# First layer of seven of nine token tiles as seven block products per pair of chunks instead of eight

## The chip, the cores and the metric

The kernel runs on one core of a Trainium2 chip. The metric is the device time of one execution in microseconds (us). Beside the times there is a profile of one execution, taken on the same core. The engines are TensorE (PE; its weight loads are shown as PEld), VectorE (DVE), ScalarE (ACT), GpSimd (POOL) and SyncE (SP), which here only issues DMAs.

## The reference

Banded attention over 8 batches, 8 heads, 576 positions and a head width of 64, then a two-layer network over all 4608 tokens. All is float32.

```
scores = (q @ k.T) / sqrt(64)
mask   = (0 <= pos_q - pos_k) & (pos_q - pos_k < 64)
attn   = softmax(where(mask, scores, -1e9))
x      = (attn @ v) as [4608 tokens, 512]
h      = x @ w_in                                  # 512 -> 2048
g      = h if h >= 1, 0 if h <= -1, else (h + 1)**2 / 4
out    = g @ w_out                                 # 2048 -> 512
```

## The kernel before

**Split operands.** Each float32 operand of a large matmul is kept as a high part and a low part that the array takes at full rate (type F32R), and a product is three matmuls: high times high, high times low, low times high. So every "block product" below is three matmuls for each 128 rows of the contraction.

**Tiles.** The tokens go in nine tiles of 512. The hidden width of 2048 is cut into NF = 16 chunks f of 128. For a tile t and a chunk f, `ffn_in` (L568) does the first layer: 4 pieces of the contraction times 3 parts = 12 matmuls of 128x512 into one PSUM bank of the pool `ps_h` (2 banks). Then the gate: ScalarE `ffn_relu` (L578) and `ffn_square` (L583), VectorE `ffn_gate` (L590, which reads the bank once more and so frees it), ScalarE `ffn_high` (L595), GpSimd `ffn_low` (L600; on VectorE in tile 0). `ffn_out` (L613) is the second layer: 12 matmuls of 128x512 into four banks `acc` that live for the whole tile. So a chunk is two blocks of 12 matmuls on PE; the blocks of different chunks alternate. In tile 0, in the first chunks of tile 1 and in the last chunk of the last tile some first-layer blocks are cut into halves of 256 columns.

**Attention.** A tile's x comes from four attention steps s of 128 tokens each, which run while the tile before it is in the network: scores on PE (L378, pool `ps_a`), mask and maximum on VectorE (L390, L394), exponentials on ScalarE (L401), division (L413, one head half on VectorE, the other on GpSimd), transposes on VectorE (L422), values on PE (L442), and then the split of x into `xh` and `xl` (L239 or L237, L455). From s = 8 on the scores of a step and the values of the step before it are one piece of work on PE (`joined`), so they stand next to each other.

**Weights.** The weights come in as int64 words holding float64, and are turned into high and low float32 parts once, in tile 0, by a chain on ScalarE and VectorE (L266 to L305). They stay in SBUF for the whole run (one slot `w{f}_{unit}` each).

**What sets the order.** The class `Plan` takes every piece of work with a key (its due time in units of a block), a cost per engine it may run on, what it needs, and which buffers it takes and gives back. It walks through time and gives each engine the next piece; the kernel's instructions are then written in that order. Each engine works through its own list strictly in that order, waiting on semaphores. SP issues all DMAs but the first two.

```
        xi = x_in[t] = add(key, dict(PE=12 * (12.5 + n * .4175)), lambda e, f=f, r=r: ffn_in(t, f, r), ...
        joined = SOON <= s < NT // SB - 1
```

Of the kernel before, what the change touches and what calls it, by code (L numbers as in the profile page):

```python
# [50 lines left out]
FIRST_LOAD = 0, (0,)  # L51
# [31 lines left out]
BUFS = dict(qt=2, kt=2, vt=4, ps_a=2, sm=4, ptd=3, x=2, u=2, ps_h=2, a=2, gh=2, gl=2, acc=4, o=2)  # L83
# [85 lines left out]
def banded_attention_then_ffn(ctx: ExitStack, tc: tile.TileContext, q, k, v, w, masks, out, dims):  # L169
# [4 lines left out]
    NF = w.shape[0]  # L174
# [6 lines left out]
    xpool = ctx.enter_context(tc.tile_pool(name="xpool", bufs=BUFS["x"]))  # L181
# [20 lines left out]
    wpool = ctx.enter_context(tc.tile_pool(name="wpool", bufs=1))  # L202

# [47 lines left out]
    def w_load(g, eng=nc.sync):  # L251
        f, units = g
        m = len(units) * DM
        ws[g] = t = wpool.tile([P, 4 * m], U16, name="raw", tag=f"w{f}_{units[0]}")
        src = w[f, :, units[0]:units[-1] + 1].bitcast(U16)
        eng.dma_start(out=t[:, :4 * m - 1], in_=src.rearrange("p u n -> p (u n)")[:, 1:])  # L256

    def w_sign(g):

        m = len(g[1]) * DM
# [21 lines left out]
    def w_rest(g):  # L284

        m = len(g[1]) * DM
# [8 lines left out]
    def w_high(g, eng):  # L295
        f, units = g
        ws[g] = t = wpool.tile([P, len(units), 2, DM], F32R, name="wts", tag=f"w{f}_{units[0]}")
        for j, u in enumerate(units):
            wts[f, u] = t[:, j]
        us[g] = us[g].bitcast(F32).rearrange("p (u n) -> p u n", n=DM)  # L300
        copy(eng, t[:, :, 0], us[g])
# [7 lines left out]
    def add_weights(f, units):  # L309
        g = f, units  # L310
        m = len(units) * DM
        act, high, join, low, small = 105 + .916 * m, 92 + .844 * m, 10 + 1.22 * m, 67 + 1.05 * m, 90 + .25 * m
        key = f * W_STEP - (W_FIRST[f] if f < len(W_FIRST) else W_LEAD) + .5 * units[0]
        x = add(W0_KEY + W0_STEP * (f + .5 * units[0]), dict(SP=W_LOAD * len(units)), lambda e: None if g == FIRST_LOAD else w_load(g), lag=DMA_LAG)
# [8 lines left out]
        for u in units:  # L323
            w_ready[f, u] = x
# [90 lines left out]
    def att_transpose(s, h, i):  # L415


        sm, pt = blk[s, h][1], ptd[(2 * s + h) % len(ptd)]
        for j in range(QB // SQ):
# [10 lines left out]
    def att_transposed(s, h, eng):  # L430
        copy(eng, ptd[(2 * s + h) % len(ptd)], pts.pop((s, h)))

    def att_values(s, pool):

        vt, pt = [vts.pop((s, i)) for i in range(2)], [ptd[(2 * s + h) % len(ptd)] for h in range(2)]
        vals[s] = ps = banks_of_heads(pool)
        for p in range(NP):
            for i in range(2):
                n = slice(i * QB, (i + 1) * QB)
                for h in range(2):  # L440
                    c = (2 * p + h) * D
                    nc.tensor.matmul(  # L442
                        ps[half[h], p, n], lhsT=vt[i][:, c:c + D], rhs=pt[h][:, p, n], start=True, stop=True
                    )

    def att_high(t, i, eng):
        s = starts[t] // SB + i
        if t not in xt:
            xt[t] = [xpool.tile([P, NP, TMAX], F32R, name=n) for n in ("xh", "xl")]
        copy(eng, xt[t][0][:, :, i * SB:(i + 1) * SB], vals[s])  # L450
# [7 lines left out]
    x_ready, x_first = {}, {}  # L458
    last = dict(s=[], t=[], v=[])

    before = {}

    def add_step(t, i):

        s = starts[t] // SB + i
        masked = s < PE_MASKS
        joined = SOON <= s < NT // SB - 1
# [20 lines left out]
        if s - 1 in before:  # L488
            needs_v, gives_v, split = before.pop(s - 1)

            def do(e):
                att_scores(s, masked, ps)
                att_values(s - 1, "ps_h")
# [14 lines left out]
        for h in range(2):  # L508
# [22 lines left out]
            else:  # L531
                if s >= SOON:
                    due = key + B_DUE[1] + B_DUE[2] * h
                x = add(
                    due, dict(DVE=1890), lambda e, h=h: att_transpose(s, h, 0), [x] + first, takes=["ptd"]
                )
                first = [x]
                taken.append(x)
                x = add(due, dict(DVE=1890), lambda e, h=h: att_transpose(s, h, 1), [x], gives=[("sm", xs, h)])
# [5 lines left out]
        def split(xo, due, pv):  # L545
            after = [xo] if i == 0 else [xo, x_first[t]]
# [11 lines left out]


# [16 lines left out]
    def ffn_relu(t, f, r):  # L576
        gs[t, f, r.start] = [gate_tile("a", F32, r)]
        nc.scalar.activation(gs[t, f, r.start][0], phs[t, f, r.start], AF.Relu, bias=0.5, scale=0.5)  # L578
# [22 lines left out]

    def ffn_out(t, f, r, i0=None):

        _, gh, gl = gs[t, f, r.start]
        for k, i in enumerate(subs(r)):
            if i0 not in (None, i):
                continue
            if f == 0:
                acc[t, i] = bank("acc")
            sub = slice(k * P, (k + 1) * P)  # L610
            for n in pieces(t, i) if f == NF - 1 else [slice(0, DM)]:
                for j, (g, part) in enumerate(((gh, 0), (gh, 1), (gl, 0))):
                    nc.tensor.matmul(  # L613
                        acc[t, i][:, n], lhsT=g[:, sub], rhs=wts[f, 1][:, part, n], start=(f == 0 and j == 0),
                        stop=(f == NF - 1 and j == 2 and n.stop == DM),
# [32 lines left out]

    def parts(t, f):
# [3 lines left out]
        key = step(t) + f * n / 384  # L653
        if t == 1 and f < FRONT:
            return [(r, step(t) + (i * FRONT + f) * m / 384) for i, r in enumerate(halves)]
# [6 lines left out]
    def add_ffn(t):  # L662
        first, before, x_out = {}, [x_in[t - 1]] if t else [], {}
        for f in range(NF):
            for r, key in parts(t, f):
                n = r.stop - r.start
                over = {x_in[t, i] for i in subs(r)} if f else set(before) | {x_ready[t][i] for i in subs(r)}
                last_in = f == NF - 1 and r.stop == TILES[t]
                xi = x_in[t] = add(
                    key, dict(PE=12 * (12.5 + n * .4175)), lambda e, f=f, r=r: ffn_in(t, f, r),  # L670
                    [w_ready[f, 0], *over] + ([x_in[t]] if last_in else []), takes=["ps_h"],
                    gives=[("x", x_first[t])] if last_in else [],
                )
                for i in subs(r):
                    x_in[t, i] = xi
                late = G_LATE if t == 0 else [0] * 5
                xa = add(key + late[0], dict(ACT=70 + n * .83), lambda e, f=f, r=r: ffn_relu(t, f, r), [xi], takes=["a"])
# [4 lines left out]
                    key + late[2], dict(DVE=65 + n * 1.04), lambda e, f=f, r=r: ffn_gate(t, f, r), [xq], gives=[("ps_h", xi)]  # L682
                )
                xh = add(key + late[3], dict(ACT=90 + n * .84), lambda e, f=f, r=r: ffn_high(t, f, r), [xg], takes=["gh"])
# [5 lines left out]
                over = {x_out[i] for i in subs(r)} if f else set()  # L690

                ends = t == len(TILES) - 1 and f == NF - 1 and r.stop == TILES[t]
                for i0 in subs(r) if ends else [None]:
                    xo = add(
                        key + O_LAG, dict(PE=3 * (n / P if i0 is None else 1) * 232), lambda e, f=f, r=r, i0=i0: ffn_out(t, f, r, i0),
                        [xl, w_ready[f, 1], *over], takes=[] if f else ["acc"] * len(subs(r)),
# [24 lines left out]
    for t in reversed(range(len(TILES))):  # L721
        for i in reversed(range(TILES[t] // SB)):
            at, apart = (step(t) - A_LEAD, A_STEP) if t < 2 else (step(t) - A_END - B_STEP, B_STEP if t > 2 else B_FIRST)
# [7 lines left out]
    for f in range(NF):  # L731
        for units in ((0,), (1,)) if f < FINE else ((0, 1),):
            add_weights(f, units)
    for t in range(len(TILES)):
        if t + 1 < len(TILES):
            for i in range(TILES[t + 1] // SB):
                add_step(t + 1, i)
        add_ffn(t)
    with tc.manual_schedule():
# [54 lines left out]
```

## Time and profile before

| | |
|---|---|
| median of 3 runs | 901.85 us (901.27 to 902.82) |
| profiled execution, first to last instruction | 899.2 us |
| what lies around that span, against the median | 2.65 us |
| PE busy | 885.6 us (98%) |
| VectorE, ScalarE, GpSimd busy | 539.3, 452.2, 192.7 us |
| a middle tile (436 to 532 us): PE, VectorE, ScalarE, GpSimd busy | 96.00, 57.65, 43.60, 24.12 of 96 us |
| granted TensorE clock, mean | 0.994 |

The profiled execution has no time of its own other than its span; the table sets the span against the median of the runs. A busy PE need not be PE at its peak, because matmuls overlap in the records; what one costs is read from the distance between the starts of neighbours, which the chain that ended last gives for whole blocks. L numbers are lines of the kernel above.

### The profile page before, as it was taken

What the parts mean: (1) busy time and instruction counts of PE and PEld (TensorE: products, weight loads), DVE (VectorE), ACT (ScalarE), POOL (GpSimd) and SP (SyncE); (2) the same over time, 40 slices, a digit from 0 to 9 for tenths busy, and PEclk for the clock granted to TensorE, in tenths of its full rate; (3) what the DMA queues carried; (4) which work ended last, traced back from release to release, by engine and by line L of the source; (5) the groups of instructions that cost most, each with busy time, mean ns of one, the idle gap of its engine ahead of it and who ended that gap; (6) DMA issues with size and microseconds to landing.
All of it is one profiled execution on the core that took longest, in us unless ns stands there. A gap on an engine that the chain in (4) does not pass through costs nothing.

```text
span 899.2 us, 17299 instructions
## 1 busy us (share of the span) xinstructions
PE 885.6 (98%) x6843; PEld 729.1 (81%) x6843; DVE 539.3 (60%) x1373; ACT 452.2 (50%) x1139; POOL 192.7 (21%) x175
## 2 busy tenths in 40 slices
PE   7899999999999999999999999999999999999997
PEld 6788888888888888888888888888888888888886
DVE  6999996667745666666645574556466666521111
ACT  6999955445534454444444454345344453433333
POOL 1000002222222222222222232222222222222221
PEclk8999999999999999999999999999999999999999
DMA  9991012112201121111211121113011220001001
GB/s 327 403 387 66 25 53 102 53 57 104 100 17 38 53 100 54 53 54 54 101 53 53 55 100 54 43 41 104 20 54 54 80 75 24 2 1 47 1 1 48
DMA packets 29426, 69.95 MB, mean 78 GB/s; under 512 B 3616, under 2 KB 3872, under 8 KB 29344
## 3 DMA queue, kind: packets, MB, share of 16 engines
q1 hardware_dynamic: 29056, 67.92, 21.4%
q8 instruction: 54, 0.88, 0.4%
q10 hardware_dynamic: 288, 0.92, 0.3%
q14 instruction: 28, 0.23, 0.1%
HBM read 59.39 MB, written 9.44 MB: 77 GB/s over the span
## 4 chain that ended last, share of the span: by engine, by line
PE 97%; DMA 1%; DVE 1%; SPq 0%; ACT 0%; issue 0%; ACTq 0%
PE acc L613 44%; PE ps_h L568 43%; PE ps_a L378 4%; PE ps_h L442 3%; DMA raw<-in_w 1%; PE ps_a L442 1%; PE acc L227 0%; PE acc L442 0%; PE ps_a L428 0%; PE ps_h L428 0%; DVE nm L394 0%; ACT sm L401 0%; SPq L256 0%; PE ps_a L372 0%; DVE sm L413 0%; PE acc L378 0%
## 5 line engine op out<-in xcount | busy, mean ns | idle before, releaser
L568 PE MATMUL ps_h<-xh,wts 128*128 128x512 f32 (+1 forms) x1200 | 380.2, 382 | 1.8 <-DVE a L590 0.9
L613 PE MATMUL acc<-wts,gh 128*128 128x512 f32 x1154 | 360.5, 394 | 0.0
L600 POOL TENSOR_TENSOR gl<-a,gh 128x512 fp32r<-128x512 f32 (+1 forms) x131 | 167.4, 1278 | 686.8 <-ACT gh L595 579.3
L590 DVE SCALAR_TENSOR_TENSOR a<-a,ps_h 128x512 f32<-128x512 f32 (+1 forms) x150 | 99.9, 667 | 285.3 <-ACT a L583 255.1
L568 PEld LDWEIGHTS ps_h<-xh,wts 128*128 128x128 f32 x1200 | 222.9, 188 | 46.3 <-DVE a L590 1.3
L613 PEld LDWEIGHTS acc<-wts,gh 128*128 128x128 f32 x1154 | 213.4, 188 | 45.4 <-issue 0.3
L568 PE MATMUL ps_h<-xl,wts 128*128 128x512 f32 (+1 forms) x600 | 228.6, 381 | 0.7 <-DVE xl L455 0.7
L578 ACT ACTIVATE a<-ps_h 128x512 f32<-128x512 f32 (+1 forms) x150 | 87.1, 581 | 275.8 <-PE ps_h L568 273.2
L422 DVE STREAM_TRANSPOSE ptd<-sm 32x128 f32<-32x128 f32 x696 | 210.7, 303 | 23.3 <-POOL sm L413 12.6
L613 PE MATMUL acc<-wts,gl 128*128 128x512 f32 x577 | 224.5, 389 | 0.0
L595 ACT CAST gh<-a 128x512 fp32r<-128x512 f32 (+1 forms) x150 | 90.4, 603 | 105.9 <-DVE a L590 96.3
L568 PEld LDWEIGHTS ps_h<-xl,wts 128*128 128x128 f32 x600 | 113.0, 188 | 22.3 <-DVE xl L455 0.9
L613 PEld LDWEIGHTS acc<-wts,gl 128*128 128x128 f32 x577 | 108.4, 188 | 23.5 <-DVE gl L600 0.2
L401 ACT ACTIVATE sm<-sm,nm 128x96 f32<-128x96 f32 (+1 forms) x256 | 93.4, 369 | 38.6 <-DVE nm L394 38.6
L583 ACT ACTIVATE a<-a 128x512 f32<-128x512 f32 (+1 forms) x148 | 91.1, 616 | 4.7
L401 ACT ACTIVATION_READ_ACCUMULATOR sm<-sm,nm 128x1 f32 x256 | 48.7, 190 | 0.0
L378 PEld LDWEIGHTS ps_a<-kt,qt 64*32 64x32 f32 (+1 forms) x2016 | 27.7, 109 | 11.8 <-issue 10.9
L394 DVE TENSOR_REDUCE nm<-sm 128x4 f32<-128x384 f32 (+1 forms) x64 | 35.8, 561 | 0.9
L378 PE MATMUL ps_a<-kt,qt 64*32 64x96 f32 (+1 forms) x2016 | 35.3, 253 | 0.0
L390 DVE SCALAR_TENSOR_TENSOR sm<-ps_a,nmsk 128x384 f32<-128x384 f32 x58 | 31.7, 548 | 0.9 <-PE ps_a L378 0.9
L442 PE MATMUL ps_h<-ptd,vt 128*64 128x64 f32 x864 | 31.1, 225 | 0.0
L442 PEld LDWEIGHTS ps_h<-ptd,vt 128*64 128x64 f32 x864 | 27.4, 138 | 3.9
(68 smaller groups left out, 376.2 us busy)
## 6 DMA issues: line engine op xcount, KB each, us to landing
vt<-in_v SPq DMA_DIRECT2D x72, 256.0 KB, 4.4
kt<-in_k SPq DMA_DIRECT2D x35, 384.0 KB, 4.5
raw<-in_w SPq DMA_DIRECT2D x12, 1023.8 KB, 10.6
qt<-in_q SPq DMA_DIRECT2D x36, 256.0 KB, 3.0
out<-o SPq DMA_DIRECT2D x32, 256.0 KB, 2.1
raw<-in_w SPq DMA_DIRECT2D x7, 511.8 KB, 6.2
out<-sm SPq DMA_DIRECT2D x3, 256.0 KB, 2.0
raw<-in_w ACTq DMA_DIRECT2D x1, 511.8 KB, 6.2
```

The lines of the kernel that those rows point to most:

```text
L378: nc.tensor.matmul(banks[h][r, p, :n], lhsT=qt[half[h], p, r], rhs=kt[half[h], p, i * m:i * m + n], start=not masked, stop=not masked or p ...
L394: nc.vector.tensor_reduce(out=nm, in_=ps if masked else sm, axis=AX.X, op=ALU.max, negate=True)
L401: nc.scalar.activation(sm[:, p, :], (ps if masked else sm)[:, p, :], AF.Exp, bias=nm[:, p:p + 1], scale=scale if masked else 1.0, accum_ou ...
L422: nc.vector.transpose(pt[(c + j) * SQ:(c + j + 1) * SQ, :, r], sm[r, :, c * SQ:(c + 1) * SQ])
L442: nc.tensor.matmul(ps[half[h], p, n], lhsT=vt[i][:, c:c + D], rhs=pt[h][:, p, n], start=True, stop=True)
L568: nc.tensor.matmul(ps, lhsT=wts[f, 0][:, part, c * P:(c + 1) * P], rhs=x[:, c, r], start=(c == 0 and j == 0), stop=(c == NP - 1 and j == 2),)
L578: nc.scalar.activation(gs[t, f, r.start][0], phs[t, f, r.start], AF.Relu, bias=0.5, scale=0.5)
L583: nc.scalar.activation(a, a, AF.Square)
L590: nc.vector.scalar_tensor_tensor(out=a, in0=a, scalar=1.0, in1=ps, op0=ALU.min, op1=ALU.max)
L595: nc.scalar.copy(g[1], g[0])
L600: engine[eng].tensor_tensor(out=g[2], in0=g[0], in1=g[1].bitcast(F32), op=ALU.subtract)
L613: nc.tensor.matmul(acc[t, i][:, n], lhsT=g[:, sub], rhs=wts[f, 1][:, part, n], start=(f == 0 and j == 0), stop=(f == NF - 1 and j == 2 and ...
```

## The change

In tiles 2 to 8 (`PLAIN = 2`) the first layer is done two chunks (a pair n, chunks 2n and 2n+1) at a time. The 512 tokens are cut into halves of 256 columns, the pair into its two chunks, and the contraction into even and odd pieces: a product of 2x2 blocks, which Strassen's scheme does with seven block products in place of eight. A block product is 2 pieces times 3 parts = 6 matmuls of 128x256. A pair was 24 matmuls of 128x512 and is 42 of 128x256.

- **Sums of weights.** Five of the seven weight operands are sums or differences of blocks. They are made once, in tile 1, on VectorE or GpSimd (`sum_whole`, `sum_sums`, `sum_low`) and ScalarE (`sum_high`), and written with the two plain blocks to DRAM (`kept`, 1.8 MB for each of eight pairs).
- **Rings.** For every tile and pair SP loads the operands back: `ring_load` A (four operands, 1 MB) and B (three, 0.75 MB), two buffers each, in slots of weights that the first layer no longer uses.
- **Sums of x.** `x_take` copies a step's x out of PSUM (it takes the place of `att_high`), `x_sums` and `x_total` form sums and differences of the halves, and `x_high`, `x_low` split seven operands. Steps of a tile run in the order 0, 2, 1, 3.
- **Putting h together.** `ffn_products` part A (four products, 24 matmuls) fills both banks of `ps_h`; then `h_first` copies two half banks to SBUF, `h_second` combines the other halves, `h_sum` adds; part B (three products, 18 matmuls) adds on to the banks; `h_middle`, `h_last` and `h_front` finish h for both chunks in SBUF. The gate reads h there, no longer from PSUM.
- **Moved.** A tile's second layer takes the chunks in the order 1, 0, 3, 2, ... (`place`), later than before (`O_AFTER`). Scores and values stay joined only up to tile 2, and the values go to `ps_a`. From step 8 on a transpose of 6 instructions is two pieces of 3. Weights from chunk 4 on are loaded and converted as pairs of one layer, not as the two layers of one chunk.

```
+PLAIN = 2
-        joined = SOON <= s < NT // SB - 1
+        joined = SOON <= s and t <= PLAIN and i < TILES[t] // SB - 1
...
+    def add_sums(n):
+        key = step(1) + 2 * n * TMAX / 384 + (S_LATE if n < 2 else S_LATER)
...
+            x0 = add(k, tt(2 * TMAX // 2, 2), lambda e, c=c: sum_whole(n, c, e), after, takes=["tmp"])
+            x = add(k, tt(5 * P, 4), lambda e, c=c: sum_sums(n, c, e), [x0])
+            xh = add(k, dict(ACT=180 + .84 * 5 * P), lambda e, c=c: sum_high(n, c, e), [x], takes=["o"])
+            x = add(k, tt(5 * P, 2), lambda e, c=c: sum_low(n, c, e), [xh])
+            x = add(k, dict(SP=1500), lambda e, c=c: sum_keep(n, c), [x], lag=DMA_LAG, gives=[("tmp", x0), ("o", xh)])
...
+    def ring_load(t, n, i):
+        rings[t, n, i] = r = wpool.tile([P, 2, 2, 4 - i, P], F32R, name="wr", tag=(IN_A, IN_B)[i][n % 2])
+        for part in range(2):
+            nc.sync.dma_start(out=r[:, part].bitcast(F32), in_=kept[n][:, part, :, R_OPS[i]])
...
+    def ffn_products(t, n, i):
...
+        todo = (
+            ((a, 0, 3, 0), (a, 1, 0, 1), (b, 0, 1, 2), (b, 1, 2, 3)),
+            ((a, 0, 2, 4), (a, 1, 0, 5), (b, 0, 1, 6)),
+        )[i]
+        for ps, c, o, k in todo:
+            for j, (part, xp) in enumerate((p, x) for _ in range(1) for p, x in ((0, 0), (0, 1), (1, 0))):
+                for cp in range(2):
+                    nc.tensor.matmul(
+                        ps[:, c * 2 * SB:(c + 1) * 2 * SB], lhsT=r[:, part, cp, o], rhs=xo[k][:, xp, cp],
...
+    def h_first(t, n, i, eng):
+        copy(eng, h_of(t, n)[:, (768, 0)[i]:(1024, 256)[i]], prods[t, n][i][:, :2 * SB])
+    def h_second(t, n, i):
+        h = h_of(t, n)[:, (768, 0)[i]:(1024, 256)[i]]
+        nc.vector.tensor_tensor(out=h, in0=h, in1=prods[t, n][i][:, 2 * SB:], op=(ALU.subtract, ALU.add)[i])
+    def h_sum(t, n, eng):
+        h = h_of(t, n)
+        engine[eng].tensor_tensor(out=h[:, :256], in0=h[:, :256], in1=h[:, 768:], op=ALU.add)
+    def h_middle(t, n, eng):
+        copy(eng, h_of(t, n)[:, 256:768], prods[t, n][0])
+    def h_last(t, n):
+        h = h_of(t, n)
+        nc.vector.tensor_tensor(out=h[:, 768:], in0=h[:, 768:], in1=prods.pop((t, n))[1][:, :2 * SB], op=ALU.add)
+    def h_front(t, n, eng):
+        h = h_of(t, n)
+        engine[eng].tensor_tensor(out=h[:, :256], in0=h[:, :256], in1=h[:, 512:768], op=ALU.add)
+        engine[eng].tensor_tensor(out=h[:, :256], in0=h[:, :256], in1=h[:, 256:512], op=ALU.subtract)
...
+        if t >= PLAIN:
+            phs[t, f, 0] = h_of(t, f // 2)[:, f % 2 * 512:f % 2 * 512 + 512]
         nc.scalar.activation(gs[t, f, r.start][0], phs[t, f, r.start], AF.Relu, bias=0.5, scale=0.5)
```

In the changed program's order below, L786 is a matmul of `ffn_products`, L902 one of `ffn_out`, L397 scores, L461 values, L802 `h_second`, L813 `h_last`, L817 and L818 `h_front`, L875 the gate, L441 the transposes, L258 a copy on VectorE. PE in a middle tile, before: a first-layer block, then a joined attention step, then the second layer.

```order
L568 MATMUL ps_h<-xl,wts 128x512
L568 MATMUL ps_h<-xh,wts 128x512
L378 MATMUL ps_a<-kt,qt 32x96 x32
L442 MATMUL ps_h<-ptd_109,vt 64x64
L442 MATMUL ps_h<-ptd_110,vt 64x64
...
L613 MATMUL acc<-wts,gh 128x512 x2
L613 MATMUL acc<-wts,gl 128x512
```

PE early in tile 5 in the change: part B of pair 1, scores, part A of pair 2, two second-layer blocks (the chunks of pair 0), values, part B of pair 2.

```order
L786 MATMUL ps_h<-xs,wr 128x256 x18
L397 MATMUL ps_a<-kt,qt 32x96 x32
L786 MATMUL ps_h<-xs,wr 128x256 x24
L902 MATMUL acc<-wts,gh 128x512 x2
L902 MATMUL acc<-wts,gl 128x512
...
L461 MATMUL ps_a<-ptd_121,vt 64x64
L461 MATMUL ps_a<-ptd_119,vt 64x64
...
L786 MATMUL ps_h<-xs,wr 128x256 x18
```

The scores and the values, neighbours before, stand apart. The part A of pair 2 follows the part B of pair 1 with only scores between them, and a little later that of pair 4 follows pair 3 with only values between; everywhere else in a middle tile at least one second-layer block of 12 stands between two parts.

VectorE in a middle tile, before (the gate reads PSUM, `ps_h`):

```order
L422 STREAM_TRANSPOSE ptd_109<-sm 32x4x32 x6
L590 SCALAR_TENSOR_TENSOR a<-a,ps_h 128x512
L408 TENSOR_SCALAR den<-den 128x4
L409 RECIPROCAL den<-den 128x4
L422 STREAM_TRANSPOSE ptd_109<-sm 32x4x32 x6
L422 STREAM_TRANSPOSE ptd_110<-sm 32x4x32 x6
```

VectorE at a like place in the change:

```order
L802 TENSOR_TENSOR h<-h,ps_h 128x256
L258 COPY h<-ps_h 128x256
L802 TENSOR_TENSOR h<-h,ps_h 128x256
L806 TENSOR_TENSOR h<-h 128x256
L813 TENSOR_TENSOR h<-h,ps_h 128x256
L817 TENSOR_TENSOR h<-h 128x256
L818 TENSOR_TENSOR h<-h 128x256
L875 SCALAR_TENSOR_TENSOR a<-a,h 128x512 x2
L409 SCALAR_TENSOR_TENSOR sm<-ps_a,nmsk 128x4x96 x2
```

The rows that put h together have joined VectorE's list, and the gate (L875) now has two inputs in SBUF, `a` and `h`.

More of the change, by code (lines that the diff above doesn't have):

```diff
@@ L295, in w_high @@
     def w_high(g, eng):
[L296 to L299, printed above, removed]
+        f, nf, u = g
+        ws[g] = t = wpool.tile([P, nf, 2, DM], F32R, name="wts", tag=f"w{f}_{u}")
+        for j in range(nf):
+            wts[f + j, u] = t[:, j]
         us[g] = us[g].bitcast(F32).rearrange("p (u n) -> p u n", n=DM)
@@ L322, in add_weights @@
         x = add(key - W_LATE[6], dict(DVE=low), lambda e: w_low(g), [x], gives=[("u", xr)])
[L323 to L324 removed]
+        for j in range(nf):
+            w_ready[f + j, unit] = x
     xt = {}
@@ L533, in add_step @@
                     due = key + B_DUE[1] + B_DUE[2] * h
[L534 to L539, printed above, removed]
+                n = QB // SQ if s >= N_SPLIT else 1
+                for j in range(2 * n):
+                    x = add(
+                        due, dict(DVE=1890 / n), lambda e, h=h, j=j, n=n: att_transpose(s, h, j // n, range(QB // SQ) if n == 1 else [j % n]),
+                        [x] + first * (not j), takes=["ptd"] * (not j), gives=[("sm", xs, h)] * (j == 2 * n - 1),
+                    )
+                    if not j:
+                        first = [x]
+                        taken.append(x)
             ready.append(x)
@@ L545, in split @@
         def split(xo, due, pv):
+            if t >= PLAIN:
+                after = [xo] if i < 2 else [xo, x_first[t, i % 2]]
+                x = add(
+                    due, dict(ACT=485, DVE=608), lambda e: x_take(t, i, e), after, takes=["u"] if i < 2 else [],
+                    gives=[(pv, xo)],
+                )
+                if i < 2:
+                    x_first[t, i] = x
+                else:
+                    add_build(t, i % 2, due, x_first[t, i % 2], x)
+                return
             after = [xo] if i == 0 else [xo, x_first[t]]
```

332 lines of the change are left out of this document (277 added, 55 removed).

## The prediction

> **What bounds the kernel now.** I read the page first, then the table by stages, then the chain that ended last.
>
> ```profile
> span 899.2 us, 17299 instructions
> PE acc L613 44%; PE ps_h L568 43%; PE ps_a L378 4%; PE ps_h L442 3%; DMA raw<-in_w 1%; PE ps_a L442 1%; PE acc L227 0%; PE acc L442 0%; PE ps_a L428 0%; PE ps_h L428 0%; DVE nm L394 0%; ACT sm L401 0%; SPq L256 0%; PE ps_a L372 0%; DVE sm L413 0%; PE acc L378 0%
> 436.00:532.00 96.00, 96.00 (x770) 78.82 (x769) 57.65 (x157) 43.60 (x117) 24.12 (x20) 1.00 0.18 64
> ```
>
> The chain is 87% the two layers on PE. The third row is a middle tile (busy PE, weight loads, VectorE, ScalarE, GpSimd; then granted clock, DMA share, GB/s): PE has no gap and the full clock; VectorE has 38 us to spare. So a microsecond off PE there is one off the span until another engine fills up or a wait opens.
>
> The chain gives blocks by their starts. A middle stretch, then one that holds first-layer blocks of 256 columns and apart steps, then the end:
>
> ```profile
> 381.15 2.72 PE acc L613 x12
> 383.88 2.72 PE ps_h L568 x12
> 386.59 0.93 PE ps_a L378 x56
> 387.52 1.08 PE ps_h L442 x32
> 388.60 2.99 PE acc L613 x12
> ...
> 129.87 2.87 PE ps_h L568 x24
> 132.74 2.75 PE acc L613 x12
> 135.49 1.08 PE ps_a L442 x32
> 136.57 2.94 PE acc L613 x12
> 139.51 2.87 PE ps_h L568 x24
> 142.38 0.93 PE ps_a L378 x57
> 143.31 2.95 PE ps_h L568 x12
> ...
> 883.51 2.72 PE acc L613 x12
> 886.23 2.87 PE ps_h L568 x24
> 889.10 5.51 PE acc L613 x27
> ```
>
> A 128x512 matmul costs 2.72 / 12 = 0.2267 us; a 128x256 one 2.87 / 24 = 0.1196, a little over half: each carries some 0.012 us that does not shrink with the columns. A middle tile is 32 blocks of 12 and 4 joined steps.
>
> **The change, part by part.**
>
> *Products.* A pair was 24 x 0.2267 = 5.44 us and becomes 42 x 0.1196 = 5.02. Over 7 tiles x 8 pairs: 56 x 0.42 = 23.4 us gained, not the eighth (38 us) that the count of columns would give.
>
> *Change of shape.* The 512-column block after a 256 one took 2.75, not 2.72. I charge 0.02 us for 112 parts: +2.2 (bounds 0 and 3.4).
>
> *Attention apart.* Joined, a step costs 0.93 + 1.08 and 0.27 more in the block behind (2.99 for 2.72): 2.28; a middle tile is thus 32 x 2.72 + 4 x 2.28 = 96.2 us. Apart, scores cost 0.93 + 0.23 (2.95) and values 1.08 + 0.22 (2.94): 2.46. Steps 11 to 34 change, 24 x 0.18: +4.3.
>
> The weight load of a 256-column matmul must hide in 0.12 us, and in the rows it does:
>
> ```profile
> L568 PEld LDWEIGHTS ps_h<-xh,wts 128*128 128x128 f32 x1200 | 222.9, 188 | 46.3 <-DVE a L590 1.3 <-DVE xh L239 1.0 <-ACT gh L595 0.2
> ```
>
> A load shows 188 ns, yet matmuls start every 119.6 ns, so loads overlap. The Trainium skill, TensorE: Matmul & The Clock Gate, part 3 (the mechanism), says a load overlaps running matmuls only when it targets another row group, and its section on LDWEIGHTS gives about 107 ns for 128 columns; by that rule a pair would go from 24 x 320 to 42 x 214 ns, 1.3 us longer, and the sum would be +73 instead of -23.4. The trace disagrees, since 107 + 107 does not fit into 119.6 (a rival below).
>
> *Putting h together, and x.* Prices:
>
> ```profile
> L590 DVE SCALAR_TENSOR_TENSOR a<-a,ps_h 128x512 f32<-128x512 f32 x138 | 95.0, 688 | 275.7 <-ACT a L583 246.8 <-POOL gl L600 27.9
> L590 DVE SCALAR_TENSOR_TENSOR a<-a,ps_h 128x256 f32<-128x256 f32 x12 | 4.9, 417 | 9.6 <-ACT a L583 8.3 <-POOL gl L600 1.3
> L455 DVE TENSOR_TENSOR xl<-ps_h,xh 128x512 fp32r<-128x512 f32 x27 | 18.4, 683 | 0.3
> L413 DVE TENSOR_TENSOR sm<-sm,den 128x384 f32<-128x384 f32 x30 | 16.7, 558 | 1.0
> L600 POOL TENSOR_TENSOR gl<-a,gh 128x512 fp32r<-128x512 f32 x125 | 163.0, 1304 | 544.4 <-ACT gh L595 436.9 <-issue 62.4 <-PE acc L613 45.1
> L600 POOL TENSOR_TENSOR gl<-a,gh 128x256 fp32r<-128x256 f32 x6 | 4.4, 738 | 142.4 <-ACT gh L595 142.4
> L413 POOL TENSOR_TENSOR sm<-sm,den 128x384 f32<-128x384 f32 x28 | 23.2, 829 | 12.5 <-DVE den L409 7.9 <-ACT a L583 4.5
> L237 ACT COPY sm<-acc 128x256 f32<-128x256 f32 x2 | 0.6, 376 | 0.1
> L237 ACT COPY o<-acc 128x512 f32<-128x512 f32 x23 | 12.7, 579 | 0.6 <-DMA out<-o 0.4
> ```
>
> From the order, VectorE's list in tile 5 gains 44 rows of 256 columns for h (0.417 each, 18.3), 2 of 512 (1.4), 11 of 256 and 4 of 512 for taking, adding and splitting x (7.3), and a square (0.7). It loses 4 low parts, 3 casts and 1 copy of 512 (5.5) and two divisions (1.1). So 57.65 + 27.7 - 6.6 = 78.8 us. PE's tile becomes 96.2 - 8 x 0.42 + 4 x 0.18 + 16 x 0.02 = 93.9. GpSimd gains 17 rows of 256, 4 of 512 and 2 divisions: about 24.1 + 19.4 = 43.5. ScalarE gains 7 copies of 256 and 9 of 512, 6 casts, less a little: about 54. All below 93.9: cost 0 on the path, as long as no wait is longer than what covers it. What hides them is the work between the parts. From one engine to the next the gate chain shows these starts:
>
> ```profile
> 399.85 0.60 ACT L578 ACTIVATE a<-ps_h 128x512 f32<-128x512 f32 x1 [2.73 <-PE ps_h L568]
> 400.48 0.63 ACT L583 ACTIVATE a<-a 128x512 f32<-128x512 f32 x1
> 401.21 0.69 DVE L590 SCALAR_TENSOR_TENSOR a<-a,ps_h 128x512 f32<-128x512 f32 x1
> 401.94 0.62 ACT L595 CAST gh<-a 128x512 fp32r<-128x512 f32 x1 [0.82 <-DVE a L590]
> 402.69 1.29 POOL L600 TENSOR_TENSOR gl<-a,gh 128x512 fp32r<-128x512 f32 x1 [3.42 <-ACT gh L595]
> ```
>
> A handover costs about 0.1; from relu to the end of the low part it takes 4.1 us. A to B: bank a is full 12 x 0.12 = 1.43 before A ends, a block (2.72) follows, and `h_first` and `h_second` need 2 x 0.42 + 0.3: 3.0 us of slack. B to A: bank a is full 0.72 before B ends; with a block between, `h_middle` (0.69 + 0.2) leaves 2.5. From B to its first second-layer block there are at least 5.44 + 2.87 = 8.3 us for 0.5 + 4.1.
>
> Tight are the two places in a tile where only scores (1.16) or values (1.30) stand between B and A: 0.72 + 1.16 - 0.89 = 1.0 us. VectorE's rows ahead of `h_middle` there can be three transposes (0.94) or a gate (0.69), and it is 84% busy. I charge 0.3 at each of 14 places: +4.2 (bounds 0, and 1.5 each, 21).
>
> *Sums of weights.* They are made in tile 1. By the order VectorE gets 21 rows of 256, 26 of 128 (0.28, on the line through its rows of 256 and 512) and 5 of 512: 19.5 us; GpSimd 27 of 256, 38 of 128 (0.455, likewise) and 11 of 512: 51.5 us.
>
> ```profile
> 147.00:244.00 97.00, 97.00 (x859) 79.53 (x858) 68.00 (x189) 46.55 (x129) 24.62 (x21) 1.00 0.20 66
> ```
>
> 68 + 19.5 and 24.6 + 51.5 both stay under 97: no cost in the stage (bound above: 3, if the waits between them grow). Behind it comes a passage with little between: tile 1's last gate has one block and scores (2.72 + 1.16) ahead of its second layer for a chain of 4.1; in tile 2 part A, scores, part B and the next part A follow each other, so that `h_middle` has 0.72 for 0.89; and VectorE has copies of the output, masks, maxima, a division and transposes (some 4.6 us) ahead of the first `h_second` in the 5.3 us of values, A and scores, some of them waiting for ScalarE. The direct shortfalls are 0.2 us together; I take 2.5 for the passage (bounds 0.2 and 6, twice the tight sums).
>
> *Rings.* 14.7 MB a tile.
>
> ```profile
> q1 hardware_dynamic: 29056, 67.92, 21.4%
> raw<-in_w SPq DMA_DIRECT2D x12, 1023.8 KB, 10.6
> ```
>
> 67.92 MB took 0.214 x 899 = 192 us, so a tile's rings take 42 of 93.9 us, beside the 18% of now. A ring is free when part A(n) ends and wanted at A(n+2): two pairs less a part, 18 us, against 10.6 for 1 MB, measured in the crowded start. Hidden: 0. SP issues them in order with the loads of q, k, v and the stores behind; those have a whole step (24 us) of lead. Weight conversion by pairs of one layer in tile 0 is the same work in another order: 0, bounds -1 and +2.
>
> *The end.* Four second-layer blocks (10.9 us) follow the last part B; the last two need 4.6 and some 6.5 us and have 5.4 and 8.2 ahead of them: 0.
>
> **Sum.** 899.2 - 23.4 + 2.2 + 4.3 + 4.2 + 2.5 = 889.0 us of span. The median stood 2.65 above the profiled span: 891.7, say 891.5.
>
> **The rivals.**
>
> *VectorE becomes the bound by waiting for GpSimd.* Once a tile the two meet:
>
> ```profile
> 726.20 0.56 DVE L413 TENSOR_TENSOR sm<-sm,den 128x384 f32<-128x384 f32 x1
> 726.34 1.57 POOL L600 TENSOR_TENSOR gl<-a,gh 128x512 fp32r<-128x512 f32 x1 [4.57 <-ACT gh L595]
> 734.41 1.29 POOL L600 TENSOR_TENSOR gl<-a,gh 128x512 fp32r<-128x512 f32 x1 [4.35 <-ACT gh L595]
> ```
>
> The GpSimd row that starts inside a VectorE row with two SBUF inputs takes 0.28 longer. No row shows the other way round. In the change VectorE has 40 such rows a tile (4 now), since the gate reads h in SBUF, and GpSimd is busy 46% of the time. At random meetings, each half a GpSimd row (0.5 us), VectorE would lose 40 x 0.46 x 0.5 = 9 us a tile: 88 of 93.9, still hidden. It bounds from 15 us on, and decides for slower from about 17.4 (the 96.2 of before). If every row waits 0.47, 18.8 us, tiles 2 to 7 take 97.6: 899.2 + 6 x 1.4 - 3.0 for tile 8 (no attention beside it) + 2.5 = 907.1 of span, 910 us. The Trainium skill, SBUF — State Buffer, section on the two separate sides, calls the pair of ports that these engines share an exclusive lock under which the later one blocks fully; the 0.28 agrees, and it speaks for this rival.
>
> *The waits at the tight places are not 0.3 but 1.0 us, and the passage costs 5.* Then 14 x 0.7 + 2.5 = 12.3 more: 904. With 0.7 each and the passage as above it is 897. For it speaks that VectorE's list is strictly in order; against it that the transposes come in threes.
>
> *Rings come late.* Half a microsecond for each of 56 pairs would give 920; the 18 us of cover speak against it.
>
> *Weight loads set the pace.* If a matmul could not follow faster than the 188 ns of its load, a pair would take 42 x 0.188 = 7.9 us, 2.5 more than before: 899 + 138 = 1037. The blocks of 24 in 2.87 all but exclude it. The rule of the Trainium skill quoted above (TensorE: Matmul & The Clock Gate) is of this kind.
>
> **Chances.** 0.2% of 901.85 is 1.8 us, about what the measurement can tell from no change. My forecast (881 to 897): 0.60. The tight places at 0.7 to 1.0: 0.18, of which 0.10 still faster and 0.08 within 0.2%. VectorE bound: 0.15. Rings: 0.06. Loads: 0.01. So faster 0.70, same 0.08, slower 0.22. The range goes from 881 (no stall, no passage and no change of shape give 899.2 - 23.4 + 4.3 + 2.65 = 882.8, and 1 us for tile 0) to 907, which leaves out the far part of the VectorE case and the rings.
>
> **What would show it.** Blocks of 24 and 18 at 2.87 and 2.15 us (else the price per matmul is wrong); first-layer stalls listed against `h` or `ps_h` with VectorE or ScalarE as releaser, about 0.3 us, two a tile; VectorE at 79 to 88 us a tile, GpSimd at 43; gates longer than 0.69 us where GpSimd runs (the lock); a gap at tile 2's start. I am wrong if a middle tile takes over 95 us, or if PE waits for a DMA.

## The result and the profile after

The changed kernel takes 946.42 us (median of 4 runs, 943.59 to 949.49), the kernel before on the same chip 901.56 (4 runs): a ratio of 1.0505, 95% interval 1.0479 to 1.0531. It is 5% slower, 55 us above my forecast and far outside its range. The profiled execution took 943.59 us.

From the page of the changed kernel: the span, busy time by engine, and the chain by line.

```profile
span 941.8 us, 20899 instructions
PE 889.8 (94%) x7839; PEld 766.9 (81%) x7839; DVE 762.1 (81%) x1800; ACT 523.7 (56%) x1322; POOL 377.6 (40%) x392
PE acc L902 23%; PE ps_h L786 18%; DVE ptd L441 9%; PE ps_h L851 5%; DVE a L875 5%; ACT sm L420 3%; PE ps_a L461 2%; PE ps_a L397 2%; DMA kept<-half 2%; DVE u L511 2%; DMA kt<-in_k 2%; ACT a L863 1%; DVE xs L527 1%; DMA out<-o 1%; DVE sm L409 1%
```

About half of the two layers' share has left the chain (87% before, 46% now), and rows of VectorE stand in it: transposes, gate, sums of x. PE's longest waits, and the longest at a part of the first layer, from the list of waits (total, times, longest):

```profile
PE acc L902 <- ACT gh L880: 15.9, 8, 4.7
PE acc L902 <- POOL gl L885: 7.5, 9, 1.6
PE ps_a L461 <- DVE ptd L441: 5.8, 6, 2.1
...
PE ps_h L786 <- DVE h L802: 2.0, 3, 1.3
```

So PE waits mainly at the second layer, for the high and low parts of gates, and little at the first, where I had charged waits.

A middle tile, from one return of its largest gap on PE to the next (span, then busy PE, weight loads, VectorE, ScalarE, GpSimd; granted clock, DMA share, GB/s):

```profile
491.13:590.77 99.64, 96.31 (x912) 84.37 (x912) 85.37 (x209) 51.85 (x137) 45.37 (x43) 0.98 0.64 207
```

PE is idle for 3.33 us of it. VectorE's 85.37 us lie inside the 79 to 88 that I gave, and it is still 14 us short of the tile. So VectorE is not the bound by its total; where PE's gap opens is what matters. VectorE's and GpSimd's rows ahead of the gap at 491 us, and PE's at it:

```profile
479.21 0.56 DVE L432 TENSOR_TENSOR sm<-sm,den 128x384 f32<-128x384 f32 x1
479.78 2.10 DVE L511 TENSOR_TENSOR u<-u 128x256 f32<-128x256 f32 x3
481.80 0.93 DVE L441 STREAM_TRANSPOSE ptd<-sm 32x128 f32<-32x128 f32 x3
482.74 1.26 DVE L258 CAST xs<-u 128x256 fp32r<-128x256 f32 x1
...
485.12 0.41 DVE L813 TENSOR_TENSOR h<-h,ps_h 128x256 f32<-128x256 f32 x1
...
486.83 1.38 DVE L527 TENSOR_TENSOR xs<-u,xs 128x256 fp32r<-128x256 f32 x1
...
491.36 1.61 DVE L875 SCALAR_TENSOR_TENSOR a<-a,h 128x512 f32<-128x512 f32 x1
```

```profile
479.35 1.57 POOL L885 TENSOR_TENSOR gl<-a,gh 128x512 fp32r<-128x512 f32 x1 [1.82 <-ACT gh L880]
481.57 0.91 POOL L527 TENSOR_TENSOR xs<-u,xs 128x256 fp32r<-128x256 f32 x1 [0.65 <-ACT xs L256]
482.56 1.29 POOL L515 TENSOR_TENSOR u<-u 128x512 f32<-128x512 f32 x1
484.68 1.12 POOL L817 TENSOR_TENSOR h<-h 128x256 f32<-128x256 f32 x1 [0.83 <-DVE h L258]
...
486.63 1.30 POOL L527 TENSOR_TENSOR xs<-u,xs 128x512 fp32r<-128x512 f32 x1
491.15 1.27 POOL L885 TENSOR_TENSOR gl<-a,gh 128x512 fp32r<-128x512 f32 x1 [3.22 <-ACT gh L880]
```

```profile
491.13 0.73 PE L902 MATMUL acc<-wts,gh 128*128 128x512 f32 x2 [1.94 <-ACT gh L880]
492.48 0.50 PE L902 MATMUL acc<-wts,gl 128*128 128x512 f32 x1 [0.62 <-POOL gl L885]
...
495.01 1.05 PE L902 MATMUL acc<-wts,gh 128*128 128x512 f32 x2
```

VectorE's sums, low parts, casts and gates, which read SBUF alone, are stretched when they begin inside a GpSimd row: the gate at 491.36 waits for the low part that began at 491.15 and takes 1.61 instead of 0.69. In tiles 2 to 8, 24 of the 112 gates begin so and take 1.18 to 1.66; the other 88 take 0.69. The transposes at 481.80 and the row at 485.12, which reads PSUM (`ps_h`), begin inside GpSimd rows too and keep their time, 0.93 and 0.41. VectorE has next to no idle time here, the stretches add up in its list, gates come late, and GpSimd and PE wait for them. After the gap the matmuls are slow too (two in 1.05 us, not 0.62).

### The profile page after: what moved, and what is told of

It is laid out like the page before. It is cut to its first block, busy times and chain, and to the rows that moved or that the text cites. A ratio compares the mean times of both kernels' runs of the same rounds, so it can differ in the third digit from the quotient of the medians.

```text
span 941.8 us, 20899 instructions
## 1 busy us (share of the span) xinstructions
PE 889.8 (94%) x7839; PEld 766.9 (81%) x7839; DVE 762.1 (81%) x1800; ACT 523.7 (56%) x1322; POOL 377.6 (40%) x392
## 4 chain that ended last, share of the span: by engine, by line
PE 51%; DVE 28%; ACT 6%; DMA 6%; issue 4%; POOL 4%; SPq 0%; ACTq 0%; DVEq 0%; POOLq 0%
PE acc L902 23%; PE ps_h L786 18%; DVE ptd L441 9%; PE ps_h L851 5%; DVE a L875 5%; ACT sm L420 3%; PE ps_a L461 2%; PE ps_a L397 2%; DMA kept<-half 2%; DVE u L511 2%; DMA kt<-in_k 2%; ACT a L863 1%; DVE xs L527 1%; DMA out<-o 1%; DVE sm L409 1%
## 5 line engine op out<-in xcount | busy, mean ns | idle before, releaser
L902 PE MATMUL acc<-wts,gh 128*128 128x512 f32 x1154 | 367.7, 400 | 18.5 <-ACT gh L880 15.9
L786 PE MATMUL ps_h<-xs,wr 128*128 128x256 f32 x2352 | 305.7, 285 | 2.5 <-DVE h L802 2.0
L786 PEld LDWEIGHTS ps_h<-xs,wr 128*128 128x128 f32 x2352 | 293.4, 192 | 15.4 <-DVE h L802 5.1
L902 PEld LDWEIGHTS acc<-wts,gh 128*128 128x128 f32 x1154 | 213.7, 193 | 60.4 <-ACT gh L880 17.7
L902 PE MATMUL acc<-wts,gl 128*128 128x512 f32 x577 | 230.1, 399 | 7.8 <-POOL gl L885 7.5
L441 DVE STREAM_TRANSPOSE ptd<-sm 32x128 f32<-32x128 f32 x696 | 210.1, 302 | 11.1
L902 PEld LDWEIGHTS acc<-wts,gl 128*128 128x128 f32 x577 | 110.6, 192 | 37.4 <-POOL gl L885 13.5
L875 DVE SCALAR_TENSOR_TENSOR a<-a,h 128x512 f32<-128x512 f32 x112 | 96.2, 859 | 30.5 <-ACT a L868 28.8
L863 ACT ACTIVATE a<-h 128x512 f32<-128x512 f32 x112 | 70.1, 626 | 64.1 <-DVE h L813 53.1
L851 PE MATMUL ps_h<-xh,wts 128*128 128x512 f32 (+1 forms) x296 | 87.8, 365 | 3.0 <-DVE a L875 1.9
L256 ACT COPY h<-ps_h 128x256 f32<-128x256 f32 (+1 forms) x102 | 46.7, 465 | 67.4 <-PE ps_h L786 67.0
L813 DVE TENSOR_TENSOR h<-h,ps_h 128x256 f32<-128x256 f32 x56 | 23.4, 419 | 69.3 <-PE ps_h L786 69.1
L851 PEld LDWEIGHTS ps_h<-xh,wts 128*128 128x128 f32 x296 | 53.8, 190 | 12.5 <-DVE a L875 2.1
L802 DVE TENSOR_TENSOR h<-h,ps_h 128x256 f32<-128x256 f32 x112 | 46.7, 417 | 11.1 <-ACT h L256 8.3
L851 PE MATMUL ps_h<-xl,wts 128*128 128x512 f32 (+1 forms) x148 | 53.7, 363 | 0.5 <-DVE xl L474 0.5
L461 PEld LDWEIGHTS ps_a<-ptd,vt 128*64 128x64 f32 x992 | 33.4, 140 | 18.2 <-DVE ptd L441 6.6
```

The lines of the kernel that those rows point to most:

```text
L256: nc.scalar.copy(dst, src)
L461: nc.tensor.matmul(ps[half[h], p, n], lhsT=vt[i][:, c:c + D], rhs=pt[h][:, p, n], start=True, stop=True)
L786: nc.tensor.matmul(ps[:, c * 2 * SB:(c + 1) * 2 * SB], lhsT=r[:, part, cp, o], rhs=xo[k][:, xp, cp], start=i == 0 and c == 0 and j == 0 an ...
L851: nc.tensor.matmul(ps, lhsT=wts[f, 0][:, part, c * P:(c + 1) * P], rhs=x[:, c, r], start=(c == 0 and j == 0), stop=(c == NP - 1 and j == 2),)
L875: nc.vector.scalar_tensor_tensor(out=a, in0=a, scalar=1.0, in1=ps, op0=ALU.min, op1=ALU.max)
L902: nc.tensor.matmul(acc[t, i][:, n], lhsT=g[:, sub], rhs=wts[f, 1][:, part, n], start=(q == 0 and j == 0), stop=(q == NF - 1 and j == 2 and ...
```

## The experiments

Times are medians of this kernel; the kernel before stood at 900.1 to 901.0 in each set. Line numbers are those of each kernel.

**GpSimd's rows only write (tiles 2 to 8).**

```
-engine[eng].tensor_tensor(out, in0, in1, op)
+# on GpSimd: two columns, then memset(out[..., 2:]) twice
```

> Order and instruction counts of every other engine stay as in the changed kernel; in tiles 2 to 8 each GpSimd row becomes a subtraction of two columns and two memsets over the rest, so that it takes about as long as before and keeps its place in the chain, but reads next to nothing from SBUF (its results are left out). Theory 1 (VectorE's rows with two SBUF inputs wait for GpSimd's reads): the gate falls from 0.89 to about 0.69 us on average, VectorE's busy time in a middle tile from 85 to about 78 us, the wait of some 6 us per tile mostly goes, a middle tile takes 94 to 96 us instead of 99.6, and the time is 915 to 927. Theory 2 (the amount of VectorE's work in the crowded stretch is enough by itself): the gate may be shorter, but a middle tile still takes 98 us or more and the time is 938 or more.

Measured: 910.21 us (908.83 and 911.60), 36.2 less. GpSimd's share of the divisions (about five rows a tile) went on reading. The order of instructions is the same, so the stretch above can be laid beside it; and a middle tile:

```profile
469.39 0.56 DVE L444 TENSOR_TENSOR sm<-sm,den 128x384 f32<-128x384 f32 x1
469.96 1.09 DVE L264 TENSOR_TENSOR u<-u 128x256 f32<-128x256 f32 x3
...
471.92 0.44 DVE L270 CAST xs<-u 128x256 fp32r<-128x256 f32 x1
...
474.44 0.40 DVE L264 TENSOR_TENSOR xs<-u,xs 128x256 fp32r<-128x256 f32 x1
...
477.99 0.69 DVE L885 SCALAR_TENSOR_TENSOR a<-a,h 128x512 f32<-128x512 f32 x1
```

```profile
531.09:624.88 93.79, 93.79 (x914) 83.21 (x912) 75.71 (x209) 51.93 (x138) 41.95 (x117) 1.00 0.69 220
```

From the division to the end of the late gate the same list takes 9.3 us instead of 13.8 (479.21 to 492.97 above). VectorE's tile falls from 85.37 to 75.71: 9.7 us of waits at a shared port, where I had estimated 9. PE has no gap, and its tile of 93.79 is the 93.9 that I had summed. Theory 1 holds, with more back than the 915 to 927 that I gave it; theory 2 is out. The Trainium skill, SBUF — State Buffer, section on who interferes with whom (under the two separate sides), says that a VectorE instruction with two SBUF inputs contends with a GpSimd instruction that reads SBUF, not with one that only writes. The gate agrees (mean of 112 rows, tiles 2 to 8):

```profile
L875 DVE SCALAR_TENSOR_TENSOR a<-a,h 128x512 f32<-128x512 f32 x112 | 96.2, 859 | 30.5 <-ACT a L868 28.8
L885 DVE SCALAR_TENSOR_TENSOR a<-a,h 128x512 f32<-128x512 f32 x112 | 77.3, 690 | 30.8 <-ACT a L878 29.2
```

The first row is of the changed kernel, the second of this one.

**Only the low parts of gates write only.** The edit above in `ffn_low` alone.

> Of GpSimd's rows in tiles 2 to 8 only the 112 low parts of gates (rows that the kernel before had too) become writes; the new rows for h and x stay as they are. The low parts are a little over half of GpSimd's busy time there. If VectorE's waits are shared out by time, about half of the 36 us come back: 922 to 932. If it is the new rows against each other (h against x), little comes back: over 937. If it is the old low parts against the gate and the new rows, nearly all: below 917.

Measured: 928.22 us, half of the 36 back; a middle tile 96.5 to 97.5. The old rows and the new ones share the blame.

**No sums of weights.**

```
-sum_whole, sum_sums, sum_high, sum_low
+nothing; sum_keep stores msk[:, 0] in their place
```

> The sums of weight blocks are not computed in tile 1 (VectorE, GpSimd and ScalarE do nothing for them; the same bytes go to DRAM from a constant tile), all else is as in the changed kernel. Theory 1 (the sums crowd VectorE and GpSimd in tile 1, so that gates and low parts come late): of some 18 us that tile 1 and the passage lost, about 15 come back; tile 2's first products start at about 238 to 243 us instead of 255, and the time is 927 to 936. Theory 2 (the passage itself, that is attention apart, the new order of the steps and the building of x, costs it): they start at 250 or later, and the time is 940 or more. Tiles 3 to 8 stay at 99 to 101 us in both.

Measured: 932.84 us (-13.6); tile 2's first products start at 244.46 instead of 255.10, and middle tiles stay at 99.6. Theory 1, a little short of the start that I gave.

**Both edits together.**

> Both edits at once: GpSimd's rows of tiles 2 to 8 only write, and the sums of weights are not computed (both results are left out). If the two losses are separate, they add: 946.4 - 36.2 - 13.6 = 896.6, within 3 us, which is some 5 us above my forecast of 891.5, and with a middle tile at 93.8 us. If they share a cause (the waits at the port in tile 1 and later), one of them is counted twice and the time is above 902. If a third loss hides under the two, it shows as a wait of PE that neither of the single runs had.

Measured: 899.50 us (8 runs, 898.06 to 901.28). The time is 2.9 above the sum, just inside the 3 us given: in the main the two losses are separate. Middle tiles take 93.8. Without both losses, the change is worth nothing against before (ratio 0.9994, 0.9979 to 1.0009).

**GpSimd only writes in tile 1 too.** The same edit for `t >= 1` and in the sums.

> As e1_write_only, and GpSimd's rows of tile 1 (its low parts and its share of the sums of weights) only write too; VectorE's share of the sums and all transfers stay. Theory 1 (tile 1 loses by the same waits at the port): 898 to 903, near the 899.5 without any sums. Theory 2 (the sums cost by their amount on VectorE and by waiting for the stores that free their buffers): 906 to 911, close to the 910.2 of e1_write_only.

Measured: 907.61 us. Theory 2: in tile 1 the port is worth 2.6 us only, no more than the spread of the runs (906.72 and 908.51, against 908.83 and 911.60). PE still waits 7.1 us for low parts there.

**As that, and no buffer waits for its store.**

```
-nc.sync.dma_start(out=k[:, 0, c, 2:6], in_=h)    # and the others
+nc.sync.dma_start(out=k[:, 0, c, 2:6], in_=msk[:, 0] broadcast)
```

> As e10_write_only_all, but the stores of the sums take a constant tile of the same size, so that no buffer of a sum has to wait for its store (the sums are computed on VectorE and ScalarE and thrown away, GpSimd's share is writes). In tile 1's trace GpSimd waits 4 to 7 us for a store, then does a row of sums, and the low part of a gate stands behind both. Theory 1 (that wait is what the sums still cost without the port): the time falls from 907.6 to 899.5 to 903 and PE's waits for low parts in tile 1 go from 7.1 to under 3 us. Theory 2 (the amount of sum work ahead of the low parts is enough): 905 to 909, waits of 5 us or more.

Measured: 901.72 us (8 runs, ratio 1.0013, 1.0000 to 1.0026), and 2.4 us of waits for low parts in tile 1. Theory 1. The changed kernel's own trace shows the mechanism, GpSimd first, then PE:

```profile
191.98 1.80 POOL L693 TENSOR_TENSOR half<-wts 128x256 f32<-128x256 f32 x2 [4.37 <-DMA kept<-half]
193.86 2.18 POOL L704 TENSOR_TENSOR half<-half 128x256 f32<-128x256 f32 x4
...
199.10 1.27 POOL L885 TENSOR_TENSOR gl<-a,gh 128x512 fp32r<-128x512 f32 x1
```

```profile
200.42 0.50 PE L902 MATMUL acc<-wts,gl 128*128 128x512 f32 x1 [1.55 <-POOL gl L885]
```

GpSimd waits 4.37 us for a store that frees the buffer of a sum, then makes up the sums (and a low part of x), and the low part that PE needs stands behind them.

**Tile 0's weight loads alone.** The changed program with no tile by block products and attention joined, so that only layout, loads and conversion by pairs are left of the change.

```
-PLAIN = 2
+PLAIN = 10
```

> The kernel before with one part of the change alone: the weights laid out and loaded by pairs of one layer, and converted so, in tile 0. No products of blocks, no sums, attention joined as before. My prediction charged 0 with bounds of -1 and +2. With the write-only rows and without the sums 899.5 us were left, some 8 over the forecast, and in that trace tile 0's matmuls stood 4 to 5 us behind those of the kernel before. Theory 1 (this reordering costs tile 0 its slack): 904 to 907. Theory 2 (tile 0 is late for another reason, such as the sums or the attention of tile 1): 899 to 903.

Measured: 904.44 us, ratio 1.0043 (1.0026 to 1.0059): 3.5 us, theory 1. PE's two waits early in tile 0, first in the changed kernel, then here; the kernel before has a single one of 0.92 in this stretch:

```profile
39.62 0.39 PE L851 MATMUL ps_h<-xh,wts 128*128 128x256 f32 x1 [1.92 <-DVE a L875]
43.94 1.10 PE L397 MATMUL ps_a<-kt,qt 64*64 64x128 f32 x32 [2.63 <-DMA kt<-in_k]
```

```profile
40.04 0.58 PE L851 MATMUL ps_h<-xh,wts 128*128 128x256 f32 x1 [2.08 <-DVE a L875]
43.74 1.10 PE L397 MATMUL ps_a<-kt,qt 64*64 64x128 f32 x32 [0.78 <-DMA kt<-in_k]
```

**Attention apart alone**, in the kernel before:

```
-        joined = SOON <= s < NT // SB - 1
+        joined = SOON <= s < 11
```

> The kernel before, with scores and values of steps 11 to 34 as two blocks instead of one, and nothing else of the change. My forecast was 24 x 0.18 = 4.3 us more: 905 to 907. If the apart order brings waits of its own (theory 2 on the loss), it is 912 or more.

Measured: 905.71 us, 4.7 over before (ratio 1.0052, 1.0029 to 1.0074). The term of 4.3 was right.

**Rings loaded once.**

> The rings are loaded for the first two pairs of tile 2 only and then used by all pairs (wrong weights, same matmuls), so some 100 MB of DMA go away; nothing else changes. Theory 1 (transfers are not in it): 943 to 949, middle tiles 99 to 101 us. Theory 2 (rings come late, or their traffic slows the engines): a fall of more than 8 us, below 938.

Measured: 944.09 us (941.28 and 946.89), no change that counts. Theory 1: the 14.7 MB a tile are hidden. In the faster kernel with both edits PE waits for no ring either.

**The same work in other orders.** First one number:

```
+        due += X_LATE    # 5 blocks, in add_build
```

> The changed kernel with one number in the planner: building x (sums, casts and low parts) is due five blocks of PE later, so that gates and transposes go ahead of it on VectorE; same rows, correct results, and no idea of the port in the model. Theory 1 (in-order list, waits heaped in one stretch): VectorE's busy time per tile stays at about 85 us, but a middle tile falls from 99.6 to 95 to 97.5 us, and the time is 918 to 935. Theory 2 (the total counts): 940 or more.

Measured: 936.16 us, between the two ranges; middle tiles alternate between 93 and 103, 97.9 on average. VectorE is busy 81.9 a tile, not the 85 that I expected, and GpSimd 46.5 to 49.7 instead of 45.4, so the split moved too. A hint for theory 1, no more. Then a planner that knows the port:

```
+port = [held["Pool" if e == "DVE" else "DVE"]] if e in self.work[i][7] else []
-could.append((max([at, idle[e]] + free), self.work[i][0], i, e))
+could.append((max([at, idle[e]] + free + port), self.work[i][0], i, e))
```

> The whole of the changed kernel's work, correct results; only the planner's model knows that rows with SBUF operands on both sides (gate, sums for h, sums, casts and low parts of x, division, sums of weights on VectorE; all of GpSimd's rows) wait for each other, and so it sets another order and splits the rows otherwise between the two engines. Theory 1 (the waits at the port, in a list that is strictly in order, are the loss): the stretched rows get shorter or fall where nobody waits, and the time is 915 to 932. Theory 2 (the loss is in the total of VectorE's time, which no order mends): 940 or more.

Measured: 927.40 us. Its middle tiles take 92.5 and 96.9 in turn, 94.7 on average, already less than the 96.1 of before. But tile 2's first products start at 268.15 instead of 255.10: ahead of them PE waits 11.0 us for transposes alone. And with due times and placements searched under that model:

> As f1_lock, with the planner's due times and placements searched under that model: sums and low parts of x on VectorE, five and three blocks later than their step; the last sums for h on VectorE; all divisions and most low parts of gates on GpSimd; sums of weights closer together. Theory 1: the waits on PE in middle tiles go to 1 to 2 us each tile, tile 1 loses less than 8 us, and the time is 896 to 908. Theory 2: 930 or more.

> As f3_order from another search: low parts of x on either engine, sums of x seven and one blocks later than their step, first sums for h on VectorE. Theory 1: 896 to 908. Theory 2: 930 or more.

Measured: 910.17 and 916.46 us, both over the 908 given. But f3_order's middle tiles all take 94.2:

```profile
530.39:624.63 94.24, 93.98 (x917) 83.40 (x912) 84.19 (x221) 52.04 (x139) 31.78 (x29) 1.00 0.67 219
```

VectorE is busy for 84.19 us here, against 85.37 in a tile of 99.64. Its total hardly moved, and 5.4 us a tile are gone: theory 2 (the total) is out. But this kernel has another split as well as another order: GpSimd is busy 31.78 us instead of 45.37, so VectorE does more of the work and waits less. Its profiled span is 11.8 us longer than with both edits above; 6.3 of that are there when tile 2's first products start (249.25 and 242.96), behind one stall of 5.9 us. Three searches that also reckon with the stores did no better:

> The whole work of the changed kernel; as f3_order, from a search whose model also lets a store and a ring take 3 us to land: sums of x on VectorE seven and three blocks late, sums for h on GpSimd, sums of whole weight blocks on VectorE. Middle tiles at 94 to 95.5 us and a shorter tile 1 give 900 to 910; if the order cannot keep clear both of the port and of the stores, it stays at the 910.2 of f3_order or above.

> As g2_order from another search: sums of x five and six blocks late, sums for h on either engine, divisions on GpSimd. 900 to 910, or no better than 910.2.

> As g2_order from a third search: sums for h on VectorE, sums of x seven and five blocks late. 900 to 910, or no better than 910.2.

Measured: 912.29, 912.78 and 913.03 us (ratios 1.0116, 1.0130 and 1.0124). The first of them (g2_order) helps to tell order from split. In this middle tile GpSimd is as busy as in the changed kernel, 45.53 us, and PE has no gap:

```profile
532.12:626.12 94.00, 94.00 (x914) 83.41 (x912) 79.43 (x204) 51.48 (x138) 45.53 (x47) 1.00 0.69 219
```

So with as much work on GpSimd, another order and choice of rows took the gap out of this tile; tiles 3 to 6 take 94.0 to 96.4. Which rows went where differs as well, so order alone is not shown. No version here with the whole work beats the kernel before.

## Why the prediction was wrong

*What held.* Blocks of 24 and 18 at 2.87 and 2.15 us, the loads overlapping, the rings hidden, attention apart (4.3 forecast, 4.7 measured), PE's tile (93.9 and 93.79), and the size of VectorE's waits at the port (9 and 9.7 a tile). That size is partly luck: casts and rows of 128x4 wait too, which I had not counted. Without the waits VectorE's tile is 75.71, where I had summed 78.8.

*The step that failed first* is the sentence "88 of 93.9, still hidden", with "cost 0 on the path, as long as no wait is longer than what covers it" ahead of it. I compared totals per tile, and spread the 9 us evenly. They fall where x is built beside a full gate chain: 4.5 us in one stretch of 14. The slack that should have covered them is in the sentence "From B to its first second-layer block there are at least 5.44 + 2.87 = 8.3 us for 0.5 + 4.1". Part B and the high part made from it, in the changed kernel, then the same two and the first use where GpSimd only writes:

```profile
478.43 2.42 PE L786 MATMUL ps_h<-xs,wr 128*128 128x256 f32 x18
490.46 0.62 ACT L880 CAST gh<-a 128x512 fp32r<-128x512 f32 x1 [2.42 <-DVE a L875]
```

```profile
468.61 2.42 PE L796 MATMUL ps_h<-xs,wr 128*128 128x256 f32 x18
477.08 0.62 ACT L890 CAST gh<-a 128x512 fp32r<-128x512 f32 x1 [0.25 <-DVE a L885]
479.21 0.63 PE L914 MATMUL acc<-wts,gh 128*128 128x512 f32 x2
```

By that sentence the high part is ready 3.2 us after part B (0.5, and 2.7 of the 4.1). It took 6.7 even without the port, because in VectorE's list other rows stand ahead of the last sums and the gates, and it was ready 1.5 us before its use. With the port it took 10.2, and PE waited 1.94. So the overlap failed in two steps: the order of the list took most of the slack, and the waits at the port the rest. In this way the rival of the port came true without VectorE being the bound, and its point of decision, 17.4 us a tile, was wrong: 9.7 were enough. Cost: 36.2 us.

*A wait was priced at its length.* In the tile above PE idles 3.33 us, but is also busy 2.52 us longer than in the tile without the port (96.31 and 93.79). The granted clock shows most of why:

```profile
490.00:492.00 2.00, 0.73 (x2) 0.30 (x2) 1.91 (x5) 0.62 (x1) 0.85 (x1) 1.00 0.77 175
492.00:494.00 2.00, 1.52 (x5) 1.26 (x6) 1.93 (x5) 0.94 (x3) 0.67 (x2) 0.81 0.90 346
494.00:496.00 2.00, 2.00 (x6) 1.52 (x6) 1.89 (x6) 0.23 (x1) 1.04 (x1) 0.50 0.01 3
496.00:498.00 2.00, 2.00 (x15) 1.90 (x14) 1.89 (x6) 0.00 (x0) 0.74 (x1) 0.84 0.04 8
```

After gaps of 1.94 and 0.62 us it falls to 0.50. What these windows lack to 1.00 (0.19, 0.50 and 0.16 of 2 us each) is 1.7 us; the other 0.8 stay open. The Trainium skill, TensorE: Matmul & The Clock Gate, Part 1, has the clock halve after an idle window of about 3.4 us; here less than that of idle time, in two pieces, was enough.

*Sums of weights* were charged 0 in the stage, with a bound of 3, since 68 + 19.5 and 24.6 + 51.5 stay under 97. They cost 13.6 (10.7 once the port is out of tiles 2 to 8). Of these 10.7 the writes in tile 1 took off 2.6 and the freed buffers 5.9; 2.2 are the rest. Only the 5.9 are clear of the spread between runs. I had priced the rows, not the stores that they wait for, nor the low parts queued behind them.

*Tile 0's weights* were charged 0 with bounds of -1 and +2: 3.5.

*The tight places* (4.2) cost nothing: with the port out of the way the middle tile has no gap. *The passage* is under-sized at 2.5: with both large losses removed, PE still idles 4.7 us between 130 and 250 us, where it had no gap before, and 2.1 for transposes just after. The 899.5 of that kernel is 8.0 above the forecast: 3.5 are tile 0's, and if the 4.2 of the tight places are taken back as well, some 8.7 remain for the passage and what is around it, beyond the 2.5 charged. These waits, 6.8 less those 2.5, explain about half. The other half stays open.

The terms add up: 899.5, and 36.2 + 13.6 for what that kernel left out, make 949.3 against 946.4.

## What to carry to other kernels

Where two engines share a port, compare what falls into one stretch of an in-order list with the slack of that stretch, not totals over a tile; and have the planner count the port, since the same work in another order and split, with as much of it on GpSimd, left a middle tile without a gap (94.0 us instead of 99.6). Price a wait of TensorE as its length plus the slow matmuls behind it (here 3.33 us a tile, and about 1.7). For work that is added off the path, list what its buffers wait for and who is queued behind it on the same engine.

## What the runs showed of the hardware

A cast with one SBUF input was held up too, by GpSimd rows that begin just before it. Where GpSimd only writes, five of the nine casts of 128x512 for x take 0.66 us and the other four 0.40 to 0.42; the five all look like this, VectorE first, then GpSimd:

```profile
425.14 0.66 DVE L270 CAST xs<-u 128x512 fp32r<-128x512 f32 x1
```

```profile
424.82 0.46 POOL L256 TENSOR_TENSOR xs<-u,xs 128x4 fp32r<-128x4 f32 x1
425.21 0.83 POOL L258 MEMSET xs<- 128x252 f32 x2
```

The cast begins 0.14 before the end of the small row that reads, and is 0.25 longer than the short ones, so it is held past that row, into the first memset. That a pure writer holds up such a cast is argued from this, not shown.

The slow clock behind a wait is a cost of its own: in f3_order the gap of 5.9 us is followed by matmuls at half the clock until about 221 us, 5 us after its end. First the rows, then the windows:

```profile
215.91 1.53 PE L406 MATMUL ps_a<-kt,qt 64*32 64x96 f32 x62 [5.90 <-DVE sm L418]
...
219.66 1.05 PE L865 MATMUL ps_h<-xh,wts 128*128 128x512 f32 x2
```

```profile
218.00:220.00 2.00, 2.00 (x6) 1.61 (x5) 1.97 (x9) 1.35 (x6) 0.00 (x0) 0.50 0.88 229
220.00:222.00 2.00, 2.00 (x8) 1.54 (x7) 1.64 (x5) 0.48 (x2) 0.83 (x1) 0.75 0.54 209
```
